# A column of 64 bytes in front of the left-hand tiles of a two-branch mixing kernel

## The chip, the cores and the metric

The kernel runs on one core of one Trainium2 chip. The metric is the device time of one execution in microseconds (us), as the median of several runs. Engines are named as in the profile: PE is the matrix engine, PEld its loads of the stationary operand, DVE the vector engine, ACT the scalar engine, POOL the engine that issues gathers, SP the one that issues plain loads and stores.

## The reference

Two branches read the same 2048 x 576 input x, and a gate of each row mixes them.

```python
def _A_ref(x, w_r, w_i):
    X = jnp.fft.rfft2(x, axes=(-2, -1)) * (w_r + 1j * w_i)
    return jnp.fft.irfft2(X, s=(S, D), axes=(-2, -1))

def _B_ref(x, w_q, k1, k2, u, v):        # H = 32 heads, E = 64 keys a side, K = 1
    q = jnp.einsum("nd,dhc->nhc", xf, w_q)
    s1 = jnp.einsum("nhd,ed->nhe", q[..., :dk], k1)
    s2 = jnp.einsum("nhd,ed->nhe", q[..., dk:], k2)
    ...                                  # the best key of each side names one of 64 * 64 rows
    ue, ve = u[top_e], v[top_e]
    act = _gelu(jnp.einsum("nd,nhkd->nhk", xf, ue))
    return jnp.einsum("nhk,nhk,nhkd->nd", g, act, ve)

g = sigmoid((x * gate_w).sum(-1, keepdims=True))
return g * _A_ref(...) + (1 - g) * _B_ref(...)
```

Branch A multiplies a two-dimensional Fourier transform by a table. Branch B finds, for each of 2048 tokens and 32 heads, the best of 64 keys twice, fetches the row of u and v that the two name, and adds v's row weighted by a gelu of the dot product with u's row.

## The kernel before

Tokens stand in 16 tiles of 128. Heads stand in 8 chunks of 4, so a chunk has 4 x 2 x 64 = 512 score columns.

**Scores.** For each chunk, `build_m` multiplies w_q by the keys, in five pieces of the 576 input columns, and leaves each piece as two tiles of 128 x 512: mh, the rounded value, and ml, what rounding left. For each token tile, `scores` then makes 14 products of 128 x 128 by 128 x 512 into one bank of PSUM. The stationary operand is a slice of 128 columns of an xt tile (the transposed input, also in two parts, in 36 tiles of 128 x 512: nine pieces by four blocks of four token tiles), and the moving operand is an mh or ml tile. These are the score products: 8 x 16 x 14 = 1792. DVE takes the maxima (line 504), ACT the signs (512), and some small operations make the row's number.

**Gathers.** For each token tile and head of a chunk, POOL issues an indirect load of 128 rows of u and v side by side (576 + 576 numbers) into a row buffer, uv. The ring has 12 of them, and one more late. Token tiles 0 to 9 are done beside the scores (`group`: dot products in line 650, sums in lines 676 and 682, or on PE as "D products", line 708, which stream the row buffer past a diagonal tile dg). Tiles 10 to 15 are done late (`quad`: dot products in line 754, products in line 769, again with dg). Their gathers start once the last chunk's scores have reached their last pair of tiles.

**The transform** (branch A) runs after the scores, in matrix products with tables (`fold`, `f2`, `f4`, `f6`, `invert`).

**Order.** Every operation is a job of a planner. The list RANK holds one rank for each job; the planner plays the ranks through and fixes one order of instructions for each engine and for the loads of SP. It also hands out the slots of all rings. Addresses play no part in it. All matrix products are issued by one helper (line 348).

**Places in SBUF.** Pools are stacked from two ends of a partition's memory. From the low end ("left"): pp, sm, gp and then sp, in whose place the late pool lb comes. From the high end ("right"): pad, xp, and then sa, in whose place the late pool la comes. The score operands stand on both sides:

```python
    for tag in ("mh", "ml"):
        ring(tag, "sp", MB - MX)
        ring(tag + "x", "sa", MX)
    for i in range(9):
        for b in range(4):
            ring(f"xt{i}_{b}", "sa" if b < 2 else "sp", 1)
```

In even chunks, pieces 0 to 2 use the rings on the right, and the profile then shows mhx and mlx; all other pieces use mh and ml on the left. Token tiles 0 to 7 read xt tiles on the right, tiles 8 to 15 on the left; the profile calls all of them xt.

The compiled kernel before has these addresses, in bytes of a partition:

| tiles | side | first address | past a multiple of 128 |
|---|---|---|---|
| ident (pp) | left | 2176 | 0 |
| dg (sm) | left | 6464 | 64 |
| uv, the 12 row buffers (gp) | left | 8640 | 64 |
| kT (gp) | left | 13248 | 64 |
| mh, ml, xt of blocks 2 and 3 (sp) | left | 72000 | 64 |
| mhx, mlx, xt of blocks 0 and 1 (sa) | right | 134016 | 0 |
| xn (xp) | right | 183168 | 0 |

A score tile is 2048 bytes, a row buffer 4608 and a slice of an xt tile 512, all multiples of 128, so the last column holds for each of a kind. In the late pool on the left, tw stands 96 past, and the t tiles that meet it in the passes of `f4` 0, 4, 64 or 68 past; xr tiles stand 0 or 64 past.

Of the kernel before, what the change touches and what calls it, by code (L numbers as in the profile page):

```python
# [12 lines left out]
F32 = mybir.dt.float32  # L13
# [7 lines left out]
P = 128  # L21
# [257 lines left out]
def tile_kernel(ctx, tc, xn, xT, x5, wqT, wq5, kT, wri, uv, gw, t_kr, t_ff, t_fv, t_tw, t_io, out):  # L279
    nc = tc.nc  # L280
    PS = bass.MemoryType.PSUM

    pools = {}
    pools["pp"] = ctx.enter_context(tc.tile_pool(name="pp", bufs=1))
    pools["sm"] = ctx.enter_context(tc.tile_pool(name="sm", bufs=2))
    pools["gp"] = ctx.enter_context(tc.tile_pool(name="gp", bufs=1))
    pad = ctx.enter_context(tc.tile_pool(name="pad", bufs=1, side="right"))
    nc.vector.memset(pad.tile([P, 24], F32, tag="pad", name="pad"), 0.0)
    pools["xp"] = ctx.enter_context(tc.tile_pool(name="xp", bufs=1, side="right"))
# [1143 lines left out]
```

## Time and profile before

| | us |
|---|---|
| median of 3 runs | 944.68 |
| lowest and highest run | 942.21, 947.41 |
| the profiled execution | 953.06 |
| its span, first to last instruction | 951.3 |

How to read a row of the profile: a group of instructions names its line, engine, operation, written tile <- read tiles and shapes, then x and the count; behind the bar stand the busy time in us and the mean of one in ns; behind the second bar the idle time of the engine just before them, and what ended it. A timeline row gives the start, the length in us, the engine and the same names. A row that begins with two times and a colon is a stretch of the execution.

### The profile page before, as it was taken

The numbers are of one execution on the slowest core, as the hardware profiler recorded it, in microseconds if no ns is written. First come the engines' busy times: TensorE is split into PE (matmuls) and PEld (weight loads), VectorE is DVE, ScalarE is ACT, GpSimd is POOL, SyncE is SP. The second block draws the span as 40 slices with busy tenths as digits, with TensorE's granted clock in tenths as the row PEclk, the third lists the DMA queues.
The fourth block names the chain that finished last, engine by engine and source line by source line (L and its number), as shares of the span: only waits on it lengthen the run. The fifth ranks groups of instructions, "written<-read, shape, count | busy, mean of one in ns | idle before, by whom it ended". The sixth has DMA issues, their size and how long they took to land.

```text
span 951.3 us, 16189 instructions
## 1 busy us (share of the span) xinstructions
PE 862.7 (91%) x5046; PEld 672.4 (71%) x5046; DVE 837.8 (88%) x2043; ACT 654.7 (69%) x2188; POOL 568.5 (60%) x516
## 2 busy tenths in 40 slices
PE   7899999999999999999999995656899879798997
PEld 7688888878877887887788784434566555566775
DVE  3679989999989889899999999899878878897886
ACT  3799996978866877587888889946457352623633
POOL 0237456557557566656657776477777657557762
PEclk9999999999999999999999998878999979899999
DMA  9679998999889989989999999999999999999998
GB/s 315 197 315 365 351 356 330 376 349 380 323 310 387 393 327 359 378 308 345 374 326 405 362 403 373 378 377 391 410 406 408 410 369 360 388 341 380 413 413 355
DMA packets 90901, 345.05 MB, mean 363 GB/s; under 512 B 10112, under 2 KB 10752, under 8 KB 90816
## 3 DMA queue, kind: packets, MB, share of 16 engines
q0 software_dynamic: 73728, 302.02, 82.8%
q1 hardware_dynamic: 17088, 42.01, 12.1%
q8 instruction: 40, 0.66, 0.3%
q14 instruction: 45, 0.37, 0.1%
HBM read 339.27 MB, written 4.72 MB: 362 GB/s over the span
## 4 chain that ended last, share of the span: by engine, by line
DVE 33%; PE 30%; DMA 18%; ACT 9%; issue 8%; POOL 2%; SPq 0%; POOLq 0%; DVEq 0%; ACTq 0%
PE p L348 30%; DMA uv<-uv,ei 12%; DVE uv L650 10%; DVE xn L682 6%; DVE xn L676 4%; DVE mx L504 3%; DMA uv<-uv,eiq 3%; POOL uv L638 2%; ACT sg L512 2%; DVE uv L754 2%; ACT xr L735 2%; ACT fl L931 1%; DVE sq L528 1%; DMA uv<-wqT 1%; DMA uv<-x 1%
## 5 line engine op out<-in xcount | busy, mean ns | idle before, releaser
L638 POOL DMA_INDIRECT uv<-uv,ei x320 | 356.5, 1114 | 264.9 <-issue 58.7
L745 POOL DMA_INDIRECT uv<-uv,eiq x192 | 211.8, 1103 | 101.2 <-PE p L348 53.3
L512 ACT ACTIVATE sg<-p,mx 128x64 bf16<-128x64 f32 x1024 | 233.1, 364 | 45.4 <-DVE mx L504 40.5
L348 PE MATMUL p<-mh,xt 128*128 128x512 f32 x768 | 262.6, 400 | 0.2 <-ACT sg L512 0.2
L650 DVE SCALAR_TENSOR_TENSOR uv<-uv,xn 128x576 f32<-128x576 f32 x320 | 237.7, 755 | 22.4 <-DMA uv<-uv,ei 22.1
L348 PE MATMUL p<-uv,dg 128*32 128x288 f32 (+1 forms) x1072 | 144.0, 429 | 37.0 <-DVE dg L760 23.2
L348 PE MATMUL p<-ml,xt 128*128 128x512 f32 x448 | 176.0, 393 | 0.0
L348 PEld LDWEIGHTS p<-mh,xt 128*128 128x128 f32 x768 | 144.2, 188 | 32.7 <-ACT sg L512 0.6
L754 DVE SCALAR_TENSOR_TENSOR uv<-uv,xr 128x576 f32<-128x576 f32 x192 | 140.9, 753 | 7.0 <-DMA uv<-uv,eiq 6.2
L348 PEld LDWEIGHTS p<-uv,dg 128*32 128x32 f32 (+1 forms) x1072 | 79.8, 136 | 82.1 <-DVE dg L760 27.9
L348 PE MATMUL p<-mhx,xt 128*128 128x512 f32 x384 | 137.0, 403 | 0.3 <-ACT sg L512 0.3
L682 DVE SCALAR_TENSOR_TENSOR xn<-uv,a,xn 128x576 f32<-128x576 f32 x121 | 98.4, 814 | 0.1
L348 PEld LDWEIGHTS p<-ml,xt 128*128 128x128 f32 x448 | 84.2, 188 | 17.8
L348 PE MATMUL p<-kT,uv 128*128 128x128 f32 x640 | 81.0, 283 | 9.2 <-ACT kT L788 5.1
L348 PEld LDWEIGHTS p<-kT,uv 128*128 128x128 f32 x640 | 79.2, 198 | 14.1 <-ACT kT L788 5.1
L676 DVE TENSOR_TENSOR xn<-uv,xn 128x576 f32<-128x576 f32 x113 | 85.5, 757 | 1.0 <-ACT uv L675 0.5
L675 ACT ACTIVATE uv<-uv,a 128x576 f32<-128x576 f32 x113 | 82.9, 780 | 3.9 <-DVE a L663 2.3
L348 PEld LDWEIGHTS p<-mhx,xt 128*128 128x128 f32 x384 | 72.6, 189 | 16.6 <-ACT sg L512 0.7
L504 DVE TENSOR_REDUCE mx<-p 128x16 f32<-128x1024 f32 x64 | 78.1, 1221 | 3.1 <-PE p L348 3.1
L523 ACT ACTIVATE sg<-sg 128x256 bf16<-128x256 bf16 x192 | 79.7, 450 | 0.6
L348 PE MATMUL p<-mlx,xt 128*128 128x512 f32 x192 | 75.6, 394 | 0.0
L735 ACT ACTIVATE xr<-xl 32x576 f32<-32x576 f32 x96 | 65.4, 681 | 3.9 <-DVE uv L650 1.9
(120 smaller groups left out, 1087.8 us busy)
## 6 DMA issues: line engine op xcount, KB each, us to landing
uv<-wqT SPq DMA_DIRECT2D x32, 512.0 KB, 6.9
uv<-uv,ei POOLq DMA_INDIRECT x320, 7.2
w<-wri SPq DMA_DIRECT2D x16, 289.0 KB, 6.9
out<-xn SPq DMA_DIRECT2D x16, 288.0 KB, 6.2
uv<-uv,eiq POOLq DMA_INDIRECT x192, 7.9
xn<-xn SPq DMA_DIRECT2D x10, 288.0 KB, 6.2
tw<-t_tw SPq DMA_DIRECT2D x9, 256.0 KB, 6.6
uv<-xT SPq DMA_DIRECT2D x8, 256.0 KB, 6.4
```

Of the source, the lines that this page charges most:

```text
L348: after("PE", nc.tensor.matmul(*args, **kw))
L504: dv(dve(1024, True), at + O_MAX + nd("m", c, tp), lambda: nc.vector.tensor_reduce(mv.ap[:, 2 * tp : 2 * tp + 2, :], ps.ap.rearrange("p a ...
L512: on("ACT", actv(sg.ap[:, j, g, :], ps.ap[:, j, g * E : g * E + E], AF.Sign, bias=mv.ap[:, 2 * tp + j, g : g + 1], scale=-1.0))
L523: ac(act(256), at + O_ADD, lambda b=b: actv(s2()[:, :, b * Q : b * Q + Q], s2()[:, :, b * Q : b * Q + Q], AF.Copy, bias=b / 4), [sg], [])
L638: on("POOL", nc.gpsimd.indirect_dma_start(out=g.ap.rearrange("p a d -> p (a d)"), out_offset=None, in_=uv, in_offset=bass.IndirectOffsetOn ...
L650: dv(0.68, at + O_DOT + nd("d", t, c), lambda k=k, g=rows[k], xk=xk: stt(g.ap[:, 0, :], g.ap[:, 0, :], 1.0, xk.ap, op0=ALU.mult, op1=ALU.m ...
L675: ac(act_by(576), at + O_SCALE + nd("v", t, c), lambda v=v, s=s: actv(v(), v(), AF.Copy, scale=s()), [(rows[k], 1)], [a])
L676: dv(dve(576), at + O_SUM + nd("v", t, c), lambda v=v: vt(y.ap, v(), y.ap, ALU.add), [y], [(rows[k], 1)])
L682: dv(0.73, at + O_SUM + nd("v", t, c), lambda v=v, s=s: stt(y.ap, v(), s(), y.ap, op0=ALU.mult, op1=ALU.add), [y], [(rows[k], 1), a])
L735: ac(0.69, at + 0.6 * j, lambda j=j, q=q: actv(xr[t][j].ap[QB * q : QB * q + QB, :], x.ap[QB * j : QB * j + QB, :], AF.Copy), [(xr[t][j], ...
L745: on("POOL", nc.gpsimd.indirect_dma_start(out=g.ap.rearrange("p a d -> p (a d)"), out_offset=None, in_=uv, in_offset=bass.IndirectOffsetOn ...
L754: dv(0.68, at + O_QDOT + nd("d", t, c), lambda j=j: stt(rows[j].ap[:, 0, :], rows[j].ap[:, 0, :], 1.0, xr[t][j].ap, op0=ALU.mult, op1=ALU. ...
```

## The change

A tile of 128 x 16 float32 numbers, 64 bytes a partition, is taken from pool gp before anything else is, and a memset fills it. It is never read. All that is stacked behind it on the left (uv, kT and the other tiles of gp, then sp, and later lb) starts 64 bytes further on. mh, ml and the left-hand xt tiles begin at 72064, a multiple of 128, and the row buffers at 8704, another. pp and sm in front of it, dg among them, and everything on the right stay where they are. The order of the instructions is the same.

```diff
     pools["pp"] = ctx.enter_context(tc.tile_pool(name="pp", bufs=1))
     pools["sm"] = ctx.enter_context(tc.tile_pool(name="sm", bufs=2))
     pools["gp"] = ctx.enter_context(tc.tile_pool(name="gp", bufs=1))
+    nc.vector.memset(pools["gp"].tile([P, 16], F32, tag="edge", name="edge"), 0.0)
     pad = ctx.enter_context(tc.tile_pool(name="pad", bufs=1, side="right"))
     nc.vector.memset(pad.tile([P, 24], F32, tag="pad", name="pad"), 0.0)
     pools["xp"] = ctx.enter_context(tc.tile_pool(name="xp", bufs=1, side="right"))
```

## The prediction

> **What bounds the kernel now.** I read the page first, then the busy times by stage, the chain of waits, and at last single products in the timeline, because the change can only act through the pace of single instructions.
>
> ```profile
> span 951.3 us, 16189 instructions
> PE 862.7 (91%) x5046; PEld 672.4 (71%) x5046; DVE 837.8 (88%) x2043; ACT 654.7 (69%) x2188; POOL 568.5 (60%) x516
> 36.00:580.00 544.00, 534.93 (x2596) 440.09 (x2597) 509.94 (x1158) 442.62 (x1653) 330.28 (x297) 1.00 0.93 350
> 580.00:951.30 371.30, 300.30 (x2303) 208.47 (x2302) 312.44 (x862) 194.02 (x495) 237.97 (x215) 0.91 0.99 387
> 450.00:500.00 50.00, 49.50 (x245) 40.71 (x244) 50.00 (x116) 42.79 (x157) 28.47 (x27) 1.00 0.96 353
> ```
>
> The last four rows are stretches: bounds and length, then busy time and number of instructions of PE, PEld, DVE, ACT and POOL, the granted clock, the busy share of the DMA engines and GB/s. Up to 580 us, while scores are made, PE is busy in 534.93 of 544 us at the full clock, DVE in 509.94, DMA at 0.93: three resources near their limit, and in 450 to 500 us DVE has no gap at all. After 580 us the DMA engines are at 0.99 and PE has room. So a faster PE helps only before 580 us, and there only where PE and not DVE or a gather ends the wait.
>
> ```profile
> by line: PE p L348 17.2%; DMA uv<-uv,ei 16.7%; DVE uv L650 15.6%; DVE xn L682 8.8%; issue 8.3%; DVE mx L504 5.3%; DVE xn L676 5.2%; POOL uv L638 3.5%; ACT sg L512 3.3%; DVE sq L528 1.8%; DMA uv<-wqT 1.7%; DMA uv<-x 1.5%; DVE im L539 1.4%; D
> 36.36 37.53 PE p L348 x182
> 212.81 42.53 PE p L348 x217
> 320.31 18.90 PE p L348 x96
> 36.36:73.89 37.53, 31.27 (x129) 24.60 (x130) 3.64 (x6) 3.17 (x5) 0.95 0.67 251
> 212.81:255.34 42.53, 32.13 (x132) 24.47 (x133) 0.00 (x0) 0.00 (x0) 1.00 0.92 344
> 320.31:339.21 18.90, 7.80 (x28) 5.20 (x28) 0.00 (x0) 0.00 (x0) 1.00 0.91 344
> ```
>
> The first row is the chain of the first 580 us: PE holds 17.2% of it, 99.8 us. The next three rows (start, length) are its long PE pieces; they sum to 98.96 us and so are nearly all of it. The last three count, in those stretches, the instructions that touch an xt tile: 129 + 132 + 28 = 289 score products of 1792. Elsewhere the chain runs over gathers and DVE.
>
> **The change part by part.** *The memset.* One more DVE instruction at the start.
>
> ```profile
> 0.82 0.08 DVE L288 MEMSET pad<- 128x24 f32 x1 [0.82 <-PEq L1422]
> 9.07 0.69 DVE L420 TENSOR_TENSOR xt<-uv,xt 128x512 fp32r<-128x512 f32 x1 [8.18 <-ACT xt L419]
> ```
>
> Its like takes 0.08 us for 24 columns, and DVE then idles 8.18 us for the first load. A second one of 16 columns, at most 0.08 us, lies in that gap: 0. Were the gap gone it would cost 0.08 us.
>
> *No instruction moves.* Order, waits and queues of SP and POOL stay; only addresses of the left-hand tiles grow by 64 bytes. Nothing new is queued behind anything.
>
> *The score products.* By the addresses of the kernel before (section above) a product has both operands on the same distance past a multiple of 128 ("matched") when m and xt lie on the same side, and 64 bytes apart ("mixed") when they don't. By the code, 4 even chunks x 16 token tiles x 9 products read mhx or mlx: 576, half with xt on the left; the other 1216 read mh or ml, half with xt on the right. The page's counts agree (768 + 448 and 384 + 192):
>
> ```profile
> L348 PE MATMUL p<-mh,xt 128*128 128x512 f32 x768 | 262.6, 400 | 0.2 <-ACT sg L512 0.2
> L348 PE MATMUL p<-ml,xt 128*128 128x512 f32 x448 | 176.0, 393 | 0.0
> L348 PE MATMUL p<-mhx,xt 128*128 128x512 f32 x384 | 137.0, 403 | 0.3 <-ACT sg L512 0.3
> L348 PE MATMUL p<-mlx,xt 128*128 128x512 f32 x192 | 75.6, 394 | 0.0
> ```
>
> So 608 are mixed with m left, 288 mixed with m right, 896 matched. The means of 393 to 403 ns hide the pace, because a product's record overlaps the next. The pace is the step from start to start in an undisturbed run: first and last product of four runs, and, for the two long ones, their stretch with the count of products.
>
> ```profile
> 87.03 0.40 PE L348 MATMUL p<-mh,xt 128*128 128x512 f32 x1
> 108.97 0.39 PE L348 MATMUL p<-mh,xt 128*128 128x512 f32 x1
> 87.00:108.98 21.98, 21.95 (x95) 17.70 (x95) 0.00 (x0) 0.00 (x0) 1.00 1.02 402
> 553.61 0.39 PE L348 MATMUL p<-mh,xt 128*128 128x512 f32 x1
> 578.11 0.39 PE L348 MATMUL p<-ml,xt 128*128 128x512 f32 x1
> 553.55:578.12 24.57, 24.57 (x110) 20.29 (x109) 0.00 (x0) 0.00 (x0) 1.00 0.99 378
> 301.44 0.39 PE L348 MATMUL p<-mlx,xt 128*128 128x512 f32 x1
> 303.71 0.39 PE L348 MATMUL p<-mhx,xt 128*128 128x512 f32 x1
> 357.21 0.40 PE L348 MATMUL p<-mhx,xt 128*128 128x512 f32 x1
> 361.80 0.39 PE L348 MATMUL p<-mhx,xt 128*128 128x512 f32 x1
> ```
>
> From 87.03 to 108.97 us stand 95 products of chunk 1 on its first token tiles (m left, xt right): 21.94 us / 94 steps = 233.4 ns. From 553.61 us, chunk 7 on its last tiles (both left; one of the 110 began before): 24.50 / 108 = 226.9 ns. From 301.44 us, chunk 4 on its first tiles (both right), 10 steps: 227.0 ns. From 357.21 us, chunk 4 on its last tiles (m right, xt left), 20 steps: 229.5 ns. Matched is quicker, whichever side: what the change does to all. Saved: 608 x 6.5 ns = 3.95 us, and 288 x 2.6 ns = 0.75 us; together 4.7 us of PE's work. A smaller end: short runs may never settle at 227 ns. With the 229.5 ns of the last run for everything now mixed, it is 608 x 3.9 ns = 2.4 us.
>
> Against this stands a rule. The Trainium skill, "TensorE: Matmul & The Clock Gate", section "Step-by-step: what each phase is for", says that PE reads its stationary and its moving operand through two independent ports, so that loading the next weights takes nothing from the running product. By it the two operands' addresses would not matter to one another, the 4.7 us would be 0, and the time 944.7 us. The trace disagrees so far (233.4 against 226.9 ns).
>
> *What of it reaches the end.* On the chain lie 289 products. In 212.81 to 255.34 us (chunk 3, nearly all m left, its first tiles xt right) I take 112 as mixed, eight token tiles of 14: 112 x 6.5 = 0.73 us. The 157 of the other two pieces at the mean saving 4.7 us / 1792 = 2.6 ns: 0.41 us. Sum 1.1 us. The other 3.6 us shorten PE where DVE or a gather is awaited; next late there are the dot products of L650 and the gathers, which keep their times.
>
> *The other left-hand operands.* D and quad products stream a row buffer past dg. Both are 64 past now; dg lies in front of the new column and stays, the row buffers move to 0. Matched becomes mixed.
>
> ```profile
> L348 PE MATMUL p<-uv,dg 128*128 128x288 f32 x304 | 84.6, 424 | 13.7 <-ACT dg L704 13.6
> L348 PE MATMUL p<-uv,dg 128*32 128x288 f32 x768 | 59.5, 431 | 23.3 <-DVE dg L760 23.2
> L348 PE MATMUL p<-t,tw 128*128 128x289 f32 x128 | 34.5, 415 | 1.9 <-DVE t L969 0.9 <-DVE t L1016 0.6 <-DVE t L970 0.5
> L348 PE MATMUL p<-mh,ident 128*128 128x256 f32 x52 | 11.7, 309 | 4.8 <-ACT mh L459 4.6
> ```
>
> Upper price: the score products' 6.5 / 226.9 = 2.9% on 84.6 + 59.5 = 144.1 us: 4.1 us. Lower price: 0; a gain is excluded, since they are matched today. The nearest row is that of t and tw, of the same type and length, whose operands lie 28 to 36 or 92 to 96 bytes off each other: 34.5 us / 128 = 270 ns busy each, no more than the 84.6 / 304 = 278 ns of matched D products. I take 0. The products with ident (52 passes on mh) turn from mixed to matched: at most 52 x 3 ns = 0.2 us, taken as 0.
>
> *DVE and DMA on moved row buffers.* Bounded by rows of today:
>
> ```profile
> L650 DVE SCALAR_TENSOR_TENSOR uv<-uv,xn 128x576 f32<-128x576 f32 x320 | 237.7, 755 | 22.4 <-DMA uv<-uv,ei 22.1
> L754 DVE SCALAR_TENSOR_TENSOR uv<-uv,xr 128x576 f32<-128x576 f32 x192 | 140.9, 753 | 7.0 <-DMA uv<-uv,eiq 6.2
> q0 software_dynamic: 73728, 302.02, 82.8%
> q1 hardware_dynamic: 17088, 42.01, 12.1%
> ```
>
> Dot products read xn at 0 in the first row, xr at 0 or 64 in the second: 755 and 753 ns, so 2 ns x 512 = 1 us either way, and 0 is taken. The gathers land 64 past, the loads of the second queue on both kinds of address: 302.02 / 82.8 = 3.65 MB and 42.01 / 12.1 = 3.47 MB for each per cent, the difference being in the sense that 64 past costs nothing. 0 again.
>
> **Sum.** 1.1 us less on the chain, 0 for the rest: 951.3 becomes 950.2 us of span. The profiled execution took 953.06 us (1.76 us around the span) and stands 0.9% over the median of the runs, 944.68 us; the saving carried over unchanged gives 943.6 us.
>
> **The rivals.**
>
> *PE alone sets the pace* (faster). For it: PE has only 9 us without work in 544 us. Against: DVE's 50.00 of 50 us, and the chain. Then all of the 4.7 us, with 0.2 us for ident, comes off: 944.7 - 4.9 = 939.8 us, or 0.52%.
>
> *Side and not distance makes the mixed products slow* (the change does not do what it says). Mixed products are also those whose operands lie on opposite sides of the memory, and the four runs can't tell the two apart. One pair of rows could: ident lies on the left at 0, so a pass with mh is mixed on one side, a pass with mhx is matched across sides.
>
> ```profile
> 86.56 0.63 PE L348 MATMUL p<-mh,ident 128*128 128x256 f32 x4
> 87.03 0.40 PE L348 MATMUL p<-mh,xt 128*128 128x512 f32 x1
> 123.05 0.63 PE L348 MATMUL p<-mhx,ident 128*128 128x256 f32 x4
> 123.53 0.39 PE L348 MATMUL p<-mh,xt 128*128 128x512 f32 x1
> ```
>
> Four passes take 0.47 and 0.48 us to the next start: too short to speak for either. Time 944.7 us. The case in which neither side nor distance counts, and the four runs differ by where they lie in their chunks, ends there as well; it is the one that the rule of the Trainium skill above stands for.
>
> *The row buffers turn D and quad products mixed* (slower). At 2.9% this costs 4.1 us of PE, and if all of it lay on the chain against 1.1 us saved, 944.7 + 3.0 = 947.7 us. It decides (over 0.5%, 4.7 us) from 4.7 + 1.1 = 5.8 us on 144.1 us, 4.0%; then 949.4 us. For it: after 580 us PE holds the longest pieces of the page's chain, and quad products are there. Against: the row of t and tw, and that these passes take 278 ns for 288 columns where a score product takes 227 ns for 512, so they read more slowly and should collide less.
>
> **How the numbers follow.** Forecast (part of the saving arrives) 0.50; PE alone 0.20; side 0.14; neither counts 0.06; slower 0.10. The runs before spread from 942.21 to 947.41 us, so 0.5% is about what can be told from no change. Faster by more than that: 0.20. Within: 0.50 + 0.14 + 0.06 = 0.70. Slower: 0.10. The predicted time is the forecast's, 943.6 us. The range runs from the case of PE alone, 939.8 us, less 0.6 us because the third run's step is read only to 1 ns (10 steps between starts given to 0.01 us; 608 x 1 ns), so 939.2 us, to the priced end of the slower case, 947.7 us; what lies beyond its deciding point is left out.
>
> **What would show it.** In the profile after, the runs that now step at 233.4 and 229.5 ns step at 227 ns; if they stay, side or rule was right. The last score product, now at 578.11 us, starts 1 to 5 us earlier. The busy time of the two uv,dg rows stays within 1 us of 84.6 and 59.5 us; 4 us more shows the slower case. L650 and L754 stay at 755 and 753 ns, and queue 0 at 82.8% of the longer or shorter span. If the score products do quicken by some 4 us and the span doesn't follow, the chain's reading holds; if it follows in full, the failed step is the share that I let arrive, and DVE's full 50 us was no limit. The prediction would be wrong altogether if one of the moved addresses sets a price that no row of today shows.

## The result, and the profile after

The changed kernel takes 942.67 us in the median of 12 runs (937.43 to 950.68). The kernel before, run beside it on the same chip, takes 948.75 us (12 runs, 942.21 to 952.64). The ratio is 0.9945, with an interval of 0.9921 to 0.9970: between 2.8 and 7.5 us are saved, 5.2 us in the middle. The forecast was 943.6 us, but from the median of the first three of these twelve runs, 944.68 us; set against 948.75 us, its 1.1 us would have given 947.6 us. The time is as forecast; the saving is some five times the forecast one. Medians and ranges in this document are of all runs of a kernel, ratios and their intervals of its fast runs alone (within 1.5% of its fastest), so where runs scatter the two need not agree.

The profiled execution after took 941.75 us, near the median. That of before took 953.06 us, more than any of the twelve timed runs, so the two traces stand 11.3 us apart, about twice what the medians do. A difference read between them is not all the work of the change.

The page of after: its span, the busy times, queue 0, and from the part on DMA issues the two gathers, with the median time from issue to landing in us at the end of the row.

```profile
span 940.0 us, 16190 instructions
PE 853.9 (91%) x5046; PEld 669.5 (71%) x5046; DVE 835.6 (89%) x2044; ACT 653.7 (70%) x2188; POOL 567.0 (60%) x516
q0 software_dynamic: 73728, 302.02, 83.5%
uv<-uv,ei POOLq DMA_INDIRECT x320, 6.7
uv<-uv,eiq POOLq DMA_INDIRECT x192, 7.4
```

The same two rows of the page before:

```profile
uv<-uv,ei POOLq DMA_INDIRECT x320, 7.2
uv<-uv,eiq POOLq DMA_INDIRECT x192, 7.9
```

Half a microsecond comes off the landing of a gather in this pair of traces. Two kernels of the experiments below show less of a difference: 7.0 and 7.7 us with the row buffers where they were (128 passes less), 7.0 and 7.5 us with them moved (all at distance 192). By stage (score stage and the rest, columns as in the prediction):

```profile
36.00:580.00 544.00, 530.78 (x2602) 440.33 (x2600) 514.92 (x1175) 447.41 (x1675) 334.28 (x301) 1.00 0.94 357
580.00:940.00 360.00, 294.99 (x2288) 204.10 (x2288) 304.81 (x845) 186.74 (x465) 232.54 (x211) 0.92 0.99 390
```

Against 534.93 us before, PE is busy 4.2 us less between 36 and 580 us, while DVE got through 5.0 us more work (514.92 against 509.94) and DMA moved 357 GB/s instead of 350. The stretch is fixed: after, its last 12 us lie behind the scores, before only 1.5 us. The runs of score products in the timeline, and the last one of all:

```profile
84.62 0.40 PE L349 MATMUL p<-mh,xt 128*128 128x512 f32 x1
105.95 0.40 PE L349 MATMUL p<-mh,xt 128*128 128x512 f32 x1
349.83 0.39 PE L349 MATMUL p<-mhx,xt 128*128 128x512 f32 x1
354.37 0.39 PE L349 MATMUL p<-mhx,xt 128*128 128x512 f32 x1
568.02 0.39 PE L349 MATMUL p<-ml,xt 128*128 128x512 f32 x1
```

Chunk 1 on the right-hand xt tiles now takes 21.33 us / 94 steps = 226.9 ns (233.4 before), chunk 4 on the left-hand ones 4.54 us / 20 steps = 227 ns (229.5 before). The last score product starts at 568.02 instead of 578.11 us, 10.1 us earlier. The groups of the other operands that the change moved, and the new memset from the timeline:

```profile
L349 PE MATMUL p<-uv,dg 128*128 128x288 f32 x304 | 84.9, 424 | 12.5 <-ACT dg L705 12.3
L349 PE MATMUL p<-uv,dg 128*32 128x288 f32 x768 | 58.9, 427 | 22.6 <-DVE dg L761 22.4
L651 DVE SCALAR_TENSOR_TENSOR uv<-uv,xn 128x576 f32<-128x576 f32 x320 | 237.3, 754 | 18.1 <-DMA uv<-uv,ei 17.8
L755 DVE SCALAR_TENSOR_TENSOR uv<-uv,xr 128x576 f32<-128x576 f32 x192 | 140.7, 754 | 3.8 <-DMA uv<-uv,eiq 3.5
0.82 0.07 DVE L287 MEMSET edge<- 128x16 f32 x1 [0.82 <-PEq L1423]
```

The D and quad products (first two rows) cost what they did, 143.8 against 144.1 us. The dot products keep their 754 ns. But behind the second bar DVE's idle time ahead of them, nearly all ended by a gather, fell from 22.4 + 7.0 = 29.4 us to 18.1 + 3.8 = 21.9 us. The chain of waits of the first 580 us looks quite different:

```profile
by line: PE p L349 44.9%; DMA uv<-uv,ei 10.4%; DVE uv L651 10.4%; DVE xn L683 4.6%; DVE xn L677 4.1%; issue 4.1%; DVE mx L505 3.7%; ACT sg L513 3.0%; DMA uv<-wqT 1.6%; DVE sq L529 1.3%; DMA uv<-x 1.3%; DVE im L540 1.3%; DMA uv<-xT 1.1%; ACT
258.56 100.95 PE p L349 x485
```

PE's share went from 17.2% to 44.9%, that of the gathers from 16.7% to 10.4%, and that of the dot products of line 651 from 15.6% to 10.4%. This looks as if the change had taken off gathers and what follows them. But the second trace of the changed kernel (the change again, below) has this chain:

```profile
by line: PE p L349 20.2%; DVE uv L651 17.4%; DMA uv<-uv,ei 13.3%; DVE xn L683 9.2%; issue 6.7%; DVE xn L677 6.1%; DVE mx L505 5.8%; ACT sg L513 2.9%; DVE sq L529 2.0%; DVE im L540 1.7%; DMA uv<-wqT 1.7%; DMA uv<-x 1.4%; ACT uv L676 1.1%; DV
```

With 20.2% for PE it is much nearer to that of before. Two executions of one kernel differ here nearly as much as the two kernels do, so the 44.9% tell nothing about the change.

### The profile page after: what moved, and what is told of

It reads as the page before. It is cut to its first block, busy times and chain, and to the rows that moved or that the text cites. A ratio compares the mean times of both kernels' runs of the same rounds, so it can differ in the third digit from the quotient of the medians.

```text
span 940.0 us, 16190 instructions
## 1 busy us (share of the span) xinstructions
PE 853.9 (91%) x5046; PEld 669.5 (71%) x5046; DVE 835.6 (89%) x2044; ACT 653.7 (70%) x2188; POOL 567.0 (60%) x516
## 4 chain that ended last, share of the span: by engine, by line
PE 49%; DVE 25%; DMA 12%; ACT 9%; issue 4%; POOL 1%; SPq 0%; DVEq 0%; ACTq 0%; POOLq 0%
PE p L349 49%; DMA uv<-uv,ei 8%; DVE uv L651 7%; DVE xn L683 3%; DVE xn L677 3%; DVE mx L505 2%; ACT sg L513 2%; ACT xr L736 2%; DVE uv L755 2%; ACT fl L932 1%; DMA uv<-wqT 1%; DVE p L439 1%; ACT uv L676 1%; DVE sq L529 1%; DVE im L540 1%
## 5 line engine op out<-in xcount | busy, mean ns | idle before, releaser
L651 DVE SCALAR_TENSOR_TENSOR uv<-uv,xn 128x576 f32<-128x576 f32 x320 | 237.3, 754 | 18.1 <-DMA uv<-uv,ei 17.8
L349 PE MATMUL p<-uv,dg 128*32 128x288 f32 (+1 forms) x1072 | 143.6, 426 | 35.0 <-DVE dg L761 22.4
L349 PEld LDWEIGHTS p<-mh,xt 128*128 128x128 f32 x768 | 144.3, 188 | 30.5 <-DVE xn L721 0.4
```

The costliest lines, as they stand in the source:

```text
L349: after("PE", nc.tensor.matmul(*args, **kw))
L651: dv(0.68, at + O_DOT + nd("d", t, c), lambda k=k, g=rows[k], xk=xk: stt(g.ap[:, 0, :], g.ap[:, 0, :], 1.0, xk.ap, op0=ALU.mult, op1=ALU.m ...
```

## The experiments

One job ran on a chip where the kernel before took 947.09 us, the two others on chips where it took 990.37 and 992.27 us, so each kernel is compared with the kernel before of its own job alone. Edits are against the changed kernel unless it is said otherwise. `edge2` is a tile like `edge`, taken first from pool sp, so that it moves the left-hand score operands and not the row buffers.

**Only the score operands move.** `edge` leaves pool gp and stands in sp:

```diff
-    nc.vector.memset(pools["gp"].tile([P, 16], F32, tag="edge", name="edge"), 0.0)
     ...
+    nc.vector.memset(pools["sp"].tile([P, 16], F32, tag="edge2", name="edge2"), 0.0)
```

> The column stands in front of pool sp alone: only mh, ml and the left-hand xt tiles move, all 1792 score products are matched; the row buffers, kT and the whole late stage keep their addresses of before, D and quad products stay matched at 64. Theory (score products' distance is the cause and PE's saving arrives in full): steps of 227 to 228 ns, ratio to before 0.9945 +/- 0.002, as with the change. Rival A (the row buffers' or late tiles' new addresses bring the gain): 1.000. Rival B (my forecast: 1.1 us on the chain): 0.999.

All score products step at 227 ns, as after. 988.44 us in the median of only six runs, too few for a ratio, against 990.37. The same kernel with twelve runs, in the third job:

> The column in front of pool sp alone, once more: the score products have the distance 0 and the pace of the change (227.8 ns), the row buffers stay 192 past a multiple of 256. Old theory: 0.9945. New theory: the 5.4 us of PE are worth about what 29.6 us taken away or added were worth per us, 0 to 0.5 us of time per us: 0.997 to 1.000; packets as before.

986.92 us against 992.27; ratio 0.9999 (0.9942 to 1.0055). No gain is seen from the pace alone, but half a per cent isn't excluded.

**The row buffers move and the score operands stay mixed.** A second column of 64 bytes:

```diff
+    nc.vector.memset(pools["sp"].tile([P, 16], F32, tag="edge2", name="edge2"), 0.0)
```

> The change and a second column of 64 bytes in front of pool sp: the row buffers and the other tiles of gp move as in the change, and the late left-hand tiles too, but mh, ml and the left-hand xt tiles stand 64 past again (moved by 128), so 608 + 288 score products are mixed as before. Theory: steps 233 and 230 ns as before, ratio 1.000 +/- 0.002. Rival A: 0.9945. D and quad products are mixed here as in the change; if that cost 2.9% of 144 us, up to 4.1 us more: 1.004.

987.70 us, ratio 1.0018 (0.9968 to 1.0068). The products did become slow, but not as expected: with m left and xt right they now step at 229 ns (88 undisturbed products of chunk 1, from 87.56 to 107.49 us), with m right and xt left at 233.3 ns, the other way round than before. Sides don't set the pace, then, and "64 bytes off a multiple of 128" is not the whole of it.

**Both operands 64 past a multiple of 128.** The kernel before, with the right-hand side moved instead of the left:

```diff
-    nc.vector.memset(pad.tile([P, 24], F32, tag="pad", name="pad"), 0.0)
+    nc.vector.memset(pad.tile([P, 8], F32, tag="pad", name="pad"), 0.0)
```

> No column; the pad on the right is 32 bytes instead of 96, so all right-hand tiles (mhx, mlx, their xt, xn, and later la) stand 64 past, as the left-hand ones do. All score products are matched, none begins on a multiple of 128. Theory (the distance between the two operands counts, not the multiple of 128): steps 227 to 228 ns, ratio 0.9945 +/- 0.002. Rival C (a multiple of 128 is needed for both): steps no better than 229 ns or so, ratio 1.000 or above.

988.18 us, ratio 0.9963 (0.9931 to 0.9995). In its timeline (first and last product of chunk 1's run with m left and xt right; then of chunk 7's with both left):

```profile
95.03 0.39 PE L348 MATMUL p<-mh,xt 128*128 128x512 f32 x1
116.86 0.40 PE L348 MATMUL p<-mh,xt 128*128 128x512 f32 x1
561.10 0.39 PE L348 MATMUL p<-mh,xt 128*128 128x512 f32 x1
585.59 0.39 PE L348 MATMUL p<-ml,xt 128*128 128x512 f32 x1
```

The first run takes 21.83 us / 94 steps = 232.2 ns, the second 24.49 / 108 = 226.8 ns. By my reading before the change both are "matched". They aren't alike, since the operands of the first lie an odd multiple of 128 apart.

**All products mixed.** The m tiles get 128 bytes more and begin 64 bytes into their slot:

```diff
-            buf(n + "x" if ... else n, [P, CW], F32R) for n in ("mh", "ml")]
+            buf(n + "x" if ... else n, [P, CW + 32], F32R, view=lambda x: x[:, 16 : 16 + CW]) for n in ("mh", "ml")]
```

> The change, with every mh, ml, mhx and mlx tile set 64 bytes into a slot of 128 bytes more: xt on multiples of 128 and m 64 past, all 1792 score products mixed, of which half stand on the same side. Theory (distance, not side): steps 233.3 ns everywhere; against the mean of 230.9 ns before that is 1792 x 2.4 = 4.3 us more of PE's work, and if PE's time arrives in full, ratio to before 1.0046, to the change 1.010. If only the share of my forecast arrives (a quarter), 1.001. Rival D (sides count): half the products at 227 ns, ratio below 1.

987.75 us, ratio 0.9990 (0.9951 to 1.0029). The runs step at 230 to 232.5 ns, not at the expected 233.3. The slots of 2176 bytes put the m tiles alternately on two distances, 64 and 192 in the table below. In the mean over undisturbed steps it is 231.3 ns against 230.9 before, 0.8 us more for 1792 products, and the time is no longer.

The paces of all these kernels fall into one order when the address of the moving operand less that of the stationary one is counted within 256 bytes:

| distance within 256 | step, ns | seen in |
|---|---|---|
| 0 | 226.7 to 227.0 | both left or both right before; all after |
| 64 | 229.5 and 229 | m right, xt left before; m left, xt right with `edge2` added |
| 128 | 232.2 and 232.9 | both at 64 past a multiple of 128 |
| 192 | 233.3 and 233.4 | m left, xt right before; m right, xt left with `edge2` added |

This made a sharper test possible: the slowest distance for every product, with the row buffers where the change puts them.

**The change again, and the change with all products at distance 192.** The first is the changed kernel without an edit. In the second an m tile lies 192 bytes into a slot of 2304 (the order is kept, with one wait more on SP in the late part):

```diff
-            buf(n + "x" if ... else n, [P, CW], F32R) for n in ("mh", "ml")]
+            buf(n + "x" if ... else n, [P, CW + 64], F32R, view=lambda x: x[:, 48 : 48 + CW]) for n in ("mh", "ml")]
```

> The change itself once more, beside the kernels that follow, on one chip. Steps 226.9 ns in runs, 227.8 ns over all. Theory (PE's saving of 4.7 to 5.4 us arrives in full): ratio to before 0.9945 +/- 0.002. Rival (a quarter arrives, as I forecast; the first comparison was chance): 0.9988.

> The change, with every m tile set 192 bytes into a slot that is 256 bytes longer: in all 1792 products the moving operand begins 192 past the stationary one, counted in 256. The runs so far showed 226.9 ns for 0, 229.0 for 64, 232.7 for 128 and 233.3 for 192, whatever the side. Expected step 233.3 ns in runs. Against the change that is 1792 x (233.3 - 227.8) = 9.9 us of PE, against before 4.4 us. Full arrival: ratio to before 1.0046 and to the change 1.010. A quarter: 1.0012 and 1.0026. If it arrives not at all: 1.000.

The change gave 941.53 us, ratio 0.9938 (0.9915 to 0.9960): the first result again. With every product at distance 192 it is 941.77 us, ratio 0.9952 (0.9921 to 0.9983). The timeline of the latter, and its stretch from 36 to 580 us:

```profile
86.38 0.39 PE L349 MATMUL p<-mh,xt 128*128 128x512 f32 x1
108.31 0.39 PE L349 MATMUL p<-mh,xt 128*128 128x512 f32 x1
573.82 0.39 PE L349 MATMUL p<-ml,xt 128*128 128x512 f32 x1
```

```profile
36.00:580.00 544.00, 540.11 (x2608) 442.66 (x2607) 512.64 (x1169) 445.67 (x1670) 334.96 (x300) 1.00 0.94 354
```

Chunk 1's run takes 21.93 us / 94 steps = 233.3 ns, and PE is busy 540.11 us, against 534.93 before and 530.78 after. PE is slower here than in the kernel before, and the gain is there all the same. **The gain does not need quicker products.** Between the two kernels of this pair lie 9.7 us of PE's work (1792 products, 233.2 against 227.8 ns in the mean over all undisturbed steps) and 0.0014 of 947 us, 1.3 us, with intervals that leave room for some 3.6 us either way.

Where the rest stays can be seen in the two traces. The last score product of the change again:

```profile
567.54 0.39 PE L349 MATMUL p<-ml,xt 128*128 128x512 f32 x1
```

It starts 6.3 us earlier than with all at distance 192 (573.82 us), but the spans are 940.1 and 941.9 us: what follows the scores takes 372.6 us in the one and 368.1 us in the other. Most of what PE gains beside the scores is lost again behind them, where DMA is busy at a share of 0.99 and 1.00. This is one trace of each.

The groups of dot products of both, first the change again, then all at distance 192:

```profile
L651 DVE SCALAR_TENSOR_TENSOR uv<-uv,xn 128x576 f32<-128x576 f32 x320 | 237.2, 754 | 17.6 <-DMA uv<-uv,ei 17.4
L755 DVE SCALAR_TENSOR_TENSOR uv<-uv,xr 128x576 f32<-128x576 f32 x192 | 140.6, 754 | 3.7 <-DMA uv<-uv,eiq 2.5 <-PE p L349 0.9
```

```profile
L651 DVE SCALAR_TENSOR_TENSOR uv<-uv,xn 128x576 f32<-128x576 f32 x320 | 237.4, 754 | 19.2 <-DMA uv<-uv,ei 19.0
L755 DVE SCALAR_TENSOR_TENSOR uv<-uv,xr 128x576 f32<-128x576 f32 x192 | 140.6, 753 | 4.4 <-DMA uv<-uv,eiq 4.3
```

DVE waits 21.3 and 23.6 us ahead of them, as after (21.9) and unlike before (29.4).

**Less work on PE, and more.** The kernel before without one of the 14 score products of each token tile and chunk (128 passes; its scores lack a correction), and with that product made twice. The first of the two:

```diff
                 for n, (xx, m) in enumerate(seq):
+                    if i == 1 and n == 2:
+                        continue
                     mm(ps.ap[:, j, :], xx.ap[:, tsl], m.ap, ...)
```

> A large dose, to measure what share of PE's time arrives: the kernel before without one of the 14 products for each token tile and chunk (the low part of x by mh of piece 1; the scores lack that correction). 128 products of 231 ns, 29.6 us less for PE in the score stage, addresses and order of all else unchanged. Full arrival: 0.969. A quarter: 0.992. If PE's time arrives in full only for the first few us and DVE and the gathers set the rest, between 0.975 and 0.99.

> The dose the other way: the kernel before with that product of piece 1 made twice for each token tile and chunk (the scores hold the correction twice). 128 products of 231 ns, 29.6 us more for PE. If PE sets the pace of the score stage: 1.031. A quarter: 1.008. A slope near 1 here beside a smaller one without the products would say that PE is at the edge of being the limit.

Without it the kernel takes 950.1 us, ratio 1.0040 (1.0013 to 1.0067); with it twice 961.99 us, 1.0157 (1.0129 to 1.0184). The stretch from 36 to 580 us of the one, then of the other:

```profile
36.00:580.00 544.00, 514.65 (x2474) 418.79 (x2474) 509.47 (x1160) 441.44 (x1651) 329.75 (x298) 0.99 0.94 352
```

```profile
36.00:580.00 544.00, 544.00 (x2661) 453.65 (x2660) 499.15 (x1132) 434.25 (x1602) 319.45 (x291) 1.00 0.92 343
```

Taking 20.3 us of busy time from PE in that stretch (514.65 against 534.93) brought nothing; the time even rose by 3 us, which I can't explain. A shift of more than half the size of the gain, 5.2 us, can thus come about here from something that no experiment named. Adding 29.6 us of work (128 x 231 ns) fills PE to 544.00 of 544 us and costs 14.9 us, half of it. So PE stands near the edge of being the bound: this much more work costs, less work gave nothing. The dot products without the 128 passes:

```profile
L652 DVE SCALAR_TENSOR_TENSOR uv<-uv,xn 128x576 f32<-128x576 f32 x320 | 237.5, 755 | 24.6 <-DMA uv<-uv,ei 24.3
L756 DVE SCALAR_TENSOR_TENSOR uv<-uv,xr 128x576 f32<-128x576 f32 x192 | 140.8, 754 | 5.9 <-DMA uv<-uv,eiq 5.2
```

They wait 24.6 + 5.9 = 30.5 us, as before (with the passes made twice, 27.6 us). With PE unburdened the gathers are as late as ever.

**Row buffers at 256 and at 128, score pace as before.** What the three kernels that kept the gain have in common are the moved row buffers and the other tiles that moved with them. Of these, mx and sg show no price in the traces. Before, then after:

```profile
L504 DVE TENSOR_REDUCE mx<-p 128x16 f32<-128x1024 f32 x64 | 78.1, 1221 | 3.1 <-PE p L348 3.1
L512 ACT ACTIVATE sg<-p,mx 128x64 bf16<-128x64 f32 x1024 | 233.1, 364 | 45.4 <-DVE mx L504 40.5 <-DVE sq L528 3.1 <-DVE a L663 1.4
```

```profile
L505 DVE TENSOR_REDUCE mx<-p 128x16 f32<-128x1024 f32 x64 | 78.1, 1220 | 0.7 <-PE p L349 0.7
L513 ACT ACTIVATE sg<-p,mx 128x64 bf16<-128x64 f32 x1024 | 232.4, 364 | 43.9 <-DVE mx L505 39.4 <-DVE sq L529 2.9 <-DVE a L664 1.4
```

That leaves the row buffers as the next suspect. Before they begin 192 past a multiple of 256 (8640), after on one (8704). Here they are moved, and the score operands go on by 256 bytes in all, which leaves every distance as before:

```diff
+    nc.vector.memset(pools["sp"].tile([P, 48], F32, tag="edge2", name="edge2"), 0.0)
```

> The column in front of pool gp, and a second one of 192 bytes in front of pool sp: the row buffers move from 192 to 0 past a multiple of 256, mh, ml and the left-hand xt tiles move by 256 bytes, so the 1792 score products keep the distances and the pace of before (608 at 192, 288 at 64, 896 at 0). New theory (gathers into row buffers that begin on multiples of 256 have shorter packets, 178 ns for 94% of them where before 47% took longer; DMA is near its limit all along): ratio to before 0.9945 +/- 0.003, median time from issue to landing 6.8 and 7.5 us as with the change. Old theory (PE's pace): 1.000.

987.76 us, ratio 0.9932 (0.9892 to 0.9971). For 128 past, `edge` gets 48 numbers and `edge2` 16:

```diff
-    nc.vector.memset(pools["gp"].tile([P, 16], F32, tag="edge", name="edge"), 0.0)
+    nc.vector.memset(pools["gp"].tile([P, 48], F32, tag="edge", name="edge"), 0.0)
     ...
+    nc.vector.memset(pools["sp"].tile([P, 16], F32, tag="edge2", name="edge2"), 0.0)
```

> As rows_256, with the two columns of 192 and 64 bytes: the row buffers stand 128 past a multiple of 256, so on a multiple of 128 alone; the score products as before. If a multiple of 128 is enough for the gathers: packets of 178 ns, ratio 0.9945. If it takes a multiple of 256, as the Trainium skill, DMA: Bandwidth & Descriptors, section How a descriptor splits into AXI transactions, has it for the start of each transaction, packets stay longer than 178 ns for about half, and the ratio is 0.998 to 1.000.

995.54 us, ratio 1.0040 (0.9996 to 1.0083). By their ratios these two say what the theory says (new place of the row buffers: gain; multiple of 128 alone: none). The last one does not:

**All tiles of the score products and the row buffers on multiples of 256.**

```diff
-    nc.vector.memset(pad.tile([P, 24], F32, tag="pad", name="pad"), 0.0)
+    nc.vector.memset(pad.tile([P, 56], F32, tag="pad", name="pad"), 0.0)
     ...
+    nc.vector.memset(pools["sp"].tile([P, 32], F32, tag="edge2", name="edge2"), 0.0)
```

> The change, with the pad on the right at 224 bytes and a column of 128 bytes more in front of pool sp: row buffers, xn and the score operands all begin on multiples of 256, score products at distance 0. The loads and stores of xn are 26 of 607 transfers, so against the change a gain of at most 0.1%: 0.994 to before if the new theory holds, and no measurable difference to the change.

986.87 us, ratio 1.0006 (0.9951 to 1.0061). Its products step as after: 24.48 us for 108 steps, 226.7 ns, in chunk 7's last run. It has its row buffers where the kernel with them at 256 has them, and by its ratio no gain.

The medians of this job say something else again. Against 992.27 us, the row buffers at 256 stand at 0.9955, all on 256 at 0.9946, row buffers at 128 at 1.0033, and the kernel in which only the scores move, with no row buffer moved, at 0.9946. The kernel before ran here from 975.43 to 1007.48 us, a spread of 3.3%. This chip settles nothing about half a per cent.

**The packets of the gathers.** Each trace holds a record of every packet; a gather of 128 rows makes 128 of 4608 bytes, 65536 in all. Worked out from these records:

| kernel | row buffers past 256 | up to 178 ns | 179 to 190 ns | mean up to 190, ns |
|---|---|---|---|---|
| before | 192 | 53.4% | 42.3% | 179.72 |
| 128 passes less | 192 | 58.0% | 37.2% | 179.52 |
| 128 passes more | 192 | 60.6% | 34.2% | 179.40 |
| only scores move (both) | 192 | 65.7% | 29.0% | 179.17, 179.15 |
| both 64 past | 192 | 66.9% | 27.1% | 179.11 |
| row buffers 128 past | 128 | 78.2% | 15.7% | 178.72 |
| after | 0 | 94.8% | 0.7% | 178.02 |
| the change again | 0 | 95.0% | 0.7% | 178.02 |
| all at distance 192 | 0 | 94.8% | 1.1% | 178.03 |
| `edge2`, all mixed, 256, all 256 | 0 | 93.4 to 93.6% | 0.8% | 178.02 |

The order is that of the addresses, whatever the score products do and whichever chip it was. On a multiple of 256, 93 to 95% of the packets take up to 178 ns; at 128 past about a fifth take longer, and at 192 past a third to nearly a half. The Trainium skill, "DMA: Bandwidth & Descriptors", section "How a descriptor splits into AXI transactions", says that the first transaction of a descriptor that doesn't begin on a multiple of 256 bytes starts at the multiple below, and that the bytes ahead of the start still cost beats. It words this for bytes that are fetched; here it is the place of landing that moved. The direction agrees; by its beats a packet 192 past would cost some 4% more (150 beats against 144, an estimate from that page), and the records show 0.6 to 1.0% in the mean.

1.7 ns x 65536 packets / 16 DMA engines is 7.0 us of each engine's time, about the size of the gain. But the sum over all packets does not show it, since the few over 250 ns (2.9 to 4.4%) weigh more: queue 0's share times the span is 787.7 us before, 784.9 after, 784.0 in the change again and 788.4 with all at distance 192, a kernel with the full gain.

Why the two slower chips don't show one answer: the dot products of the row buffers at 256 and, below, of the second kernel in which only scores move, both of the third job:

```profile
L652 DVE SCALAR_TENSOR_TENSOR uv<-uv,xn 128x576 f32<-128x576 f32 x320 | 236.6, 751 | 18.5 <-DMA uv<-uv,ei 13.8 <-issue 4.6
L756 DVE SCALAR_TENSOR_TENSOR uv<-uv,xr 128x576 f32<-128x576 f32 x192 | 140.0, 752 | 1.2 <-DMA uv<-uv,eiq 1.0
```

```profile
L651 DVE SCALAR_TENSOR_TENSOR uv<-uv,xn 128x576 f32<-128x576 f32 x320 | 236.5, 751 | 14.7 <-DMA uv<-uv,ei 11.0 <-issue 3.6
L755 DVE SCALAR_TENSOR_TENSOR uv<-uv,xr 128x576 f32<-128x576 f32 x192 | 140.1, 752 | 2.1 <-DMA uv<-uv,eiq 1.3 <-issue 0.7
```

They wait 19.7 us with the buffers on 256, and 16.8 us with the buffers where they were before. In these two traces DVE's wait for gathers is not longer with the old place, and is short in both. On the pages, DMA holds 18% of the chain before and 20% with 128 passes less, 12 to 15% in the three traces with the gain, and 5 to 12% in all eight traces of the slower chips. There something else costs some 45 us, and may cover a few nanoseconds in a packet. I did not find what it is. Most of it lies behind the scores: the last score product starts at 580 to 591 us there (568 to 578 in the kernels of the quicker chips, the passes made twice aside), and from it to the end pass 393 to 402 us (368 to 375).

**What is shown and what is open.** Shown: the gain is there with products slower than before, and the quicker products bring 0.7 us of the 5.2 us by the pair (1.3 of 9.7 us, scaled to 5.4 us) and about half of it at the far end of the interval. Packets into row buffers on 256 are shorter. DVE waits 6 to 9 us less for gathers in the three traces with the gain (21.3 to 23.6 us) than in the two with the old place and no added work (29.4 and 30.5 us).

Not shown is that the packets make the gain. The row buffers were not moved by themselves on a chip like the first; kT and other tiles of gp, the late pool and the tiles in sp moved with them, and the 3 us of the kernel with less work on PE are unexplained as well. On the slower chips four kernels have the new place with ratios of 0.9932, 0.9990, 1.0006 and 1.0018, and one with the old place (both at 64) has 0.9963, so 0.9932 alone proves little.

## Why the prediction was right, and where it was not

The time fell into the range and near its middle, but that is partly luck: the base of 944.68 us was 4 us below the median of the twelve runs, the saving was forecast some 4 us too small, and the two errors cancel. Of the three signs, "within 0.5%" had 0.70; the ratio of 0.9945 lies just beyond it, in the case that had 0.20, with its interval on both sides of the border. By the number alone the rival "PE alone" (0.52%) came nearest, and the experiments speak against its mechanism. Step by step:

- **The memset.** 0.07 us at 0.82 us, in the gap. Right.
- **No instruction moves.** Right: 5046 passes of PE and 516 of POOL as before, and one instruction more on DVE.
- **The score products.** All step at 226.7 to 227.0 ns, as foreseen. In the mean over undisturbed steps 230.87 became 227.83 ns, 5.4 us for 1792 products against the 4.7 us taken. The independence of the two ports, which the Trainium skill states in "TensorE: Matmul & The Clock Gate", section "Step-by-step: what each phase is for", does not make the step independent of the two addresses here: 226.8 and 232.2 ns stand in one kernel (both at 64), for products of the same shapes. My rule of multiples of 128 was wrong too, and gave the right answer for this change by luck, because its operands come to lie on a distance of 0 within 256 as well.
- **The share that arrives.** A quarter was taken, 1.1 of 4.7 us. The pair that differs in the pace (and in the length of the m slots) gave 1.3 of 9.7 us, with an interval from nothing to about a half. Nothing speaks against the step. The chain that it was read from, with 17.2% for PE, is weak support, since two traces of the changed kernel have 44.9% and 20.2%.
- **D and quad products.** 143.8 against 144.1 us: 0, as taken, and the slower rival is out. But "matched becomes mixed" was not what happened to them. Counted within 256, a D product reads at 128 (first half of a row) and 0 (second half, 1152 bytes on) before, and at 192 and 64 after. By the steps of the score products that is a price of 0.7% (an estimate from the table of distances), 0.6 us of the 84.6 us, and 0.3 us more was measured (84.9).
- **DVE and DMA on the moved row buffers: the step that failed.** For DVE 0 was right (754 ns, 754 ns). For the gathers I took 0 from 3.65 against 3.47 MB per per cent of two queues. Such a quotient mixes packets of several sizes and their long stragglers, and a difference of 5% between two queues can't exclude one of 1% between two places of the same packet. The traces showed 179.7 ns becoming 178.0 ns, landings of 7.2 and 7.9 us becoming 6.7 and 7.4, and DVE's waits 7.5 us shorter, part of which may come from the long execution (953.06 us) that was traced before. This is the case that the last sentence of the prediction named, a moved address whose price no row of before shows. Whether it is the packets or something else that moved with them stays open: the term that was put at nothing is not yet shown to be the one that pays.
- **The sign that would have misled.** "If it follows in full, the failed step is the share that I let arrive." The span did follow in full (5.2 us for 5.4 us on PE), and the chain turned to PE. Still that reading is not borne out: with PE slower than before the gain remained. Two savings of the same size in one change can't be told apart in its trace. The start of the last score product, 10.1 us earlier where 1 to 5 were expected, hinted that something else had quickened; but part of it may come from the long execution traced before, and without the 128 passes it starts at 573.29 us, 4.8 us earlier, with no gain at all.

## What to carry to other kernels

A shift of a pool moves everything that is stacked behind it, so each kind of tile in it needs its own price, transfers into it included; where the page has no row for it, undo the part alone in an experiment. Take a suspected gain away again with the rest of the change left in: one kernel with the slowest pace everywhere settled here what no reading of before and after could. Trace one kernel twice before reading a difference between two chains of waits. Where gathers are awaited, let their buffers begin on multiples of 256 bytes and see whether the wait ahead of their first reader gets shorter.

## What the runs showed of the hardware

A score product of 512 columns steps at 226.7 to 233.4 ns, and in all runs measured the step goes by the distance of its two operands' addresses within 256 bytes, in the order 0, 64, 128, 192, whichever side of the memory they lie on (two runs or more for each distance; 128 and 192 differ by 0.4 to 1.2 ns only). A 4608-byte packet takes, in the mean of those up to 190 ns, 178.0 ns on a multiple of 256, 178.7 ns at 128 past and 179.1 to 179.7 ns at 192 past. And in a stage with three resources near their limit the chain of waits had 44.9% PE in one execution and 20.2% in another of the same kernel: it tells which wait came last in one execution, not what the stage would be worth without it.
